# Loading the first quarter of W1 ahead of the last v rows, and moving one batch's transposes between others: a sliding-window attention with a two-layer network behind it

## The chip, the cores and the metric

The kernel runs on one core of one Trainium2 chip. The metric is the time of one execution on the device in microseconds (us). The engines: PE (TensorE) multiplies matrices, and transposes by multiplying with an identity; DVE (VectorE) and ACT (ScalarE) do elementwise work and empty PSUM, the memory that PE writes; POOL (GpSimd) casts the inputs from f32 to f16; SP's queue issues the loads.

## The reference, cut to what matters

```python
def _attn_ref(q, k, v):                       # 8 batches, 8 heads, 576 rows, 64 wide
    scores = scale * np.matmul(q, k.transpose(0, 1, 3, 2))
    mask = (rel >= 0) & (rel < window)        # window = 64
    ...                                       # softmax over the masked scores
    return np.matmul(attn, v)

def _moe_ref(x, g_ln, w_ch1, w_ch2):          # x: 8 x 576 x 512, w_ch1: 512 x 2048
    xn = (x - mu) / np.sqrt(var + 1e-06) * g_ln
    return x + np.maximum(xn @ w_ch1, 0.0) @ w_ch2
```

## The kernel before

Batches go through PE one behind the other. While PE works on the two layers of batch g, the attention of batch g+1 is put between its pieces ("units"): `at(i, f, ...)` puts a call into **slot** i, which runs after unit i. PE runs all of this in the order written. For batch 0 there are 30 units: 8 of the first layer on half the rows, 8 on all rows, 10 of the second layer on three row blocks at once, and 4 on the last block.

```python
load_qk(0, 0); load_v(0, 0, 2)                # SP's queue, in this order
load_qk(0, 1); load_v(0, 2, 4)
for i in range(8): w1_load(i)                 # W1 in eight half-loads of 512 KB
# ...
cast_v(0, 2, 3); cast_v(0, 3, 4)              # POOL, in this order
nc.gpsimd.tensor_copy(out=vB[0][64:128, 3, :, 0:D], in_=v32[0][0:64, 3])
for i in range(8): w1_cast(i)                 # times g_ln, to f16
# ...
def t_main(b, x, half, eng=None):             # q (x=0) or k (x=1): 8 transposes, then one copy
    tp = t_tile([128, 8, 128], ...)           # slots 17 to 24: ONE shared PSUM bank
    ...                                       # also taken by zt_step, the row transposes
# batch 0's slots, which carry batch 1's attention:
at(20, b_step, 1, 1)                          # attention product, division, statistics, z
at(21, zt_step, 1, 0); at(23, zt_step, 1, 1)
at(24, t_main, 1, 0, 1, 0); at(26, t_main, 1, 1, 1, 1)
at(25, vB_cur, 1, 2, 0); at(25, vB_prev, 1, 2, 1); at(26, vB_cur, 1, 3, 0)
at(28, s_mm, 1, 2); at(28, s_mask, 1, 2)      # scores and exponentials; mask
at(29, s_mm, 1, 3); at(29, s_mask, 1, 3)
at(30, b_step, 1, 2)
# batch 1's slots:
at(1, b_step, 1, 3); at(2, zt_step, 1, 2)
at(14, b_step, 2, 0)                          # batch 2's first attention product
```

The softmax here doesn't subtract the row's maximum and nothing guards it: scores larger than these inputs give would overflow.

## Time and profile before

| | before |
|---|---|
| time, median of 3 | 308.18 us (307.89 to 308.82) |
| span of the profiled run | 305.9 us |
| PE busy | 97% |
| PE's waits after its first one | 1.9 us, all before 57 us |
| PE starts batch 0's fifth hidden unit | 25.87 us |
| batch 1's second q half landed | 46.90 us |

The lines that carry this are in the prediction. One habit of reading matters throughout: a profile names as waits only idle time of an engine. Where I speak below of a PE **stand**, I took the start-to-start distance of two products less the usual one (0.216 us for 512 columns, 0.109 for 256, 0.055 for 128), so a stand reads 0.1 to 0.2 us longer than the idle time in the wait lines. Distances up to 0.1 us over the usual, which come with every change from one kind of product to another, are not counted.

### The profile page before, as it was taken

What the parts mean: (1) busy time and instruction counts of PE and PEld (TensorE: products, weight loads), DVE (VectorE), ACT (ScalarE), POOL (GpSimd) and SP (SyncE); (2) the same over time, 40 slices, a digit from 0 to 9 for tenths busy, and PEclk for the clock granted to TensorE, in tenths of its full rate; (3) what the DMA queues carried; (4) which work ended last, traced back from release to release, by engine and by line L of the source; (5) the groups of instructions that cost most, each with busy time, mean ns of one, the idle gap of its engine ahead of it and who ended that gap; (6) DMA issues with size and microseconds to landing.
All of it is one profiled execution on the core that took longest, in us unless ns stands there. A gap on an engine that the chain in (4) does not pass through costs nothing.

```text
span 305.9 us, 7582 instructions
## 1 busy us (share of the span) xinstructions
PE 295.4 (97%) x3061; PEld 196.4 (64%) x3061; DVE 220.6 (72%) x412; ACT 150.7 (49%) x253; POOL 173.3 (57%) x256
## 2 busy tenths in 40 slices
PE   6989999999999999999999999999999999999992
PEld 4557545687454478547854786469646854788882
DVE  0778696767766995589656965896669685789972
ACT  2586635587227733775157527752475046306500
POOL 7589676564952789179806983698146507014300
PEclk9999999999999999999999999999999999999998
DMA  8999999999776997899189997993790399003014
GB/s 191 266 385 301 314 366 286 303 284 236 150 181 228 243 172 147 280 280 127 35 243 303 204 160 245 298 155 70 215 175 19 53 189 208 19 17 139 0 38 103
DMA packets 113669, 58.35 MB, mean 191 GB/s; under 512 B 83617, under 2 KB 104609, under 8 KB 113634
## 3 DMA queue, kind: packets, MB, share of 16 engines
q1 hardware_dynamic: 112576, 54.67, 74.0%
q0 software_dynamic: 768, 2.80, 3.8%
q8 instruction: 24, 0.39, 0.5%
q10 hardware_dynamic: 290, 0.40, 0.5%
q14 instruction: 11, 0.09, 0.1%
HBM read 38.80 MB, written 9.44 MB: 158 GB/s over the span
## 4 chain that ended last, share of the span: by engine, by line
PE 89%; SPq 4%; DMA 2%; POOL 1%; ACT 1%; DVE 1%; issue 0%; ACTq 0%
PE hps L401 30%; PE pA L478 12%; PE pB L478 8%; PE pC L478 8%; PE hph L537 6%; PE ch L413 6%; PE xps L321 4%; PE sc L286 4%; PE ch L554 3%; PE tp L229 3%; PE lA L592 2%; DMA w1s<-in_moe_w_ch_dram 2%; SPq L141 2%; POOL w1g L190 1%; SPq L89 1%; PE lC L592 1%
## 5 line engine op out<-in xcount | busy, mean ns | idle before, releaser
L401 PE MATMUL hps<-zT,w1g 128*128 128x512 f16 x416 | 95.3, 380 | 0.0
L405 ACT ACTIVATE hrT<-hps 128x512 f16<-128x512 f32 x104 | 62.3, 599 | 39.3 <-PE hps L401 35.7
L401 PEld LDWEIGHTS <-w1g 128*128 128x128 f16 x416 | 38.6, 98 | 43.3 <-issue 0.7
L294 ACT ACTIVATE pt<-sc 128x512 f16<-128x512 f32 x72 | 39.0, 594 | 27.7 <-PE sc L286 20.5
L478 PEld LDWEIGHTS <-sS 128*128 128x128 f16 x448 | 43.4, 98 | 4.9
L351 POOL TENSOR_SCALAR rsz<-mvg 128x1 f32<-128x1 f32 x28 | 10.2, 364 | 60.6 <-DVE mvg L332 59.8
L128 POOL CAST qk<-qk 128x1024 f16<-128x1024 f32 x32 | 36.3, 1147 | 11.3 <-DMA qk<-in_k_dram 5.6
L478 PEld LDWEIGHTS <-hrT 128*128 128x128 f16 x336 | 32.4, 98 | 5.5 <-ACT hrT L637 0.3
L301 DVE TENSOR_TENSOR pt<-pt,mask 128x1024 f16<-128x1024 f16 x32 | 27.5, 867 | 8.4 <-ACT pt L294 8.4
L215 ACT COPY qkT<-tp 128x1024 f16<-128x1024 f16 x16 | 16.1, 1012 | 34.1 <-PE tp L229 34.1
L485 DVE TENSOR_TENSOR xn<-pA,xn 128x512 f32<-128x512 f32 x28 | 19.2, 685 | 16.7 <-PE pA L478 11.1
L478 PE MATMUL pC<-w2s,sS 128*128 128x256 f16 x224 | 27.1, 273 | 0.0
L478 PE MATMUL pA<-wT,sS 128*128 128x256 f16 x224 | 26.9, 273 | 0.0
L354 POOL TENSOR_SCALAR z<-xn,rsz 128x512 f16<-128x512 f32 x28 | 24.9, 888 | 2.9
L327 DVE TENSOR_TENSOR xn<-xps,rcp 128x512 f32<-128x512 f32 x36 | 24.9, 691 | 1.5 <-DMA out_dram<-xn 0.3
L329 DVE BATCH_NORM_STATS2 stats<-xn 128x6 f32<-128x512 f32 x36 | 25.0, 695 | 1.2
L324 DVE RECIPROCAL rcp<-xps 128x8 f32<-128x8 f32 x36 | 7.3, 204 | 24.7 <-PE xps L321 24.7
L452 DVE TENSOR_TENSOR sS<-hrT 128x512 f16<-128x512 f16 (+1 forms) x40 | 24.5, 613 | 0.6 <-ACT hrT L405 0.6
L537 PE MATMUL hph<-zT,w1g 128*128 128x256 f16 x192 | 23.8, 273 | 1.0 <-DVE zT L371 0.5
L321 PEld LDWEIGHTS <-pt 128*64 128x64 f16 x576 | 12.2, 110 | 13.7 <-issue 5.5
L352 POOL TENSOR_TENSOR rsz<-rsz,mhalf 128x1 f32<-128x1 f32 x28 | 19.4, 692 | 2.3
L147 POOL CAST vA<-v 128x1024 f16<-128x1024 f32 (+2 forms) x19 | 17.4, 930 | 5.6 <-DMA v<-in_v_dram 5.6
(113 smaller groups left out, 448.9 us busy)
## 6 DMA issues: line engine op xcount, KB each, us to landing
out_dram<-xn SPq DMA_DIRECT2D x33, 256.0 KB, 2.8
qk<-in_q_dram SPq DMA_DIRECT2D x16, 512.0 KB, 6.2
qk<-in_k_dram SPq DMA_DIRECT2D x16, 512.0 KB, 6.9
v<-in_v_dram SPq DMA_DIRECT2D x32, 256.0 KB, 7.7
w2s<-in_moe_w_ch_dram SPq DMA_DIRECT2D x9, 512.0 KB, 9.2
w1s<-in_moe_w_ch_dram SPq DMA_DIRECT2D x4, 512.0 KB, 7.3
tk<-in_k_dram SPq DMA_DIRECT2D x8, 256.0 KB, 4.5
tv<-in_v_dram SPq DMA_DIRECT2D x8, 256.0 KB, 5.0
```

Of the source, the lines that this page charges most:

```text
L128: nc.gpsimd.tensor_copy(out=dst[:, :].rearrange("p (a j) e d -> p a e j d", j=j), in_=t[:, :].rearrange("p (a e j d) -> p a e j d", e=2, j ...
L294: nc.scalar.activation(out=o, in_=i, func=AF.Exp, bias=0.0, scale=scale)
L301: nc.vector.tensor_tensor(out=ptv, in0=ptv, in1=mb, op=ALU.mult)
L321: nc.tensor.matmul(out=xps[64 * r:64 * r + 64, h, :D + 1], lhsT=pt[:, par, hp, r, :], rhs=rhs, start=True, stop=True)
L327: nc.vector.tensor_tensor(out=xn, in0=xps[:, :, 0:D], in1=rcp_b, op=ALU.mult)
L329: nc.vector.bn_stats(out=stats, in_=xv)
L354: nc.gpsimd.tensor_scalar(out=z, in0=xv, scalar1=rs, scalar2=nm, op0=ALU.mult, op1=ALU.add)
L401: nc.tensor.matmul(out=hps, lhsT=w1g[:, kc, 128 * hc:128 * (hc + 1)], rhs=zT[g][:, kc, :], start=(kc == 0), stop=(kc == NKC - 1),)
L405: nc.scalar.activation(out=hrT[:, hc, :], in_=hps, func=AF.Relu, bias=0.0, scale=1.0)
L452: nc.vector.tensor_tensor(out=o, in0=x, in1=y, op=op)
L478: nc.tensor.matmul(out=o, lhsT=a[:, c, 128 * p:128 * p + 128], rhs=wv[:, c, :], start=(first and (p == 0 or split_c) and c == 0), stop=(c ...
L537: nc.tensor.matmul(out=hps[:, e], lhsT=w1g[:, kc, 128 * hc:128 * (hc + 1)], rhs=zT[g][:, kc, 256 * half:256 * half + 256], start=(kc == 0) ...
```

## The change

It has two parts. Part 1: two of the eight half-loads of W1 come before the last 128 rows of batch 0's v, in SP's queue and on POOL, so that PE's first hidden unit need not wait for weights. Part 2: the transposes of batch 1's second half go two slots earlier, between the row transposes, and its scores one slot earlier, so that PE does not run out of work at the end of batch 0.

```diff
     load_qk(0, 1)
-    load_v(0, 2, 4)
-    for i in range(8):
+    load_v(0, 2, 3)
+    w1_load(0)
+    w1_load(1)
+    load_v(0, 3, 4)
+    for i in range(2, 8):
         w1_load(i)
...
     cast_v(0, 2, 3)
+    w1_cast(0)
+    w1_cast(1)
     cast_v(0, 3, 4)
     nc.gpsimd.tensor_copy(out=vB[0][64:128, 3, :, 0:D], in_=v32[0][0:64, 3])
-    for i in range(8):
+    for i in range(2, 8):
         w1_cast(i)
...
-            at(24, t_main, 1, 0, 1, 0)
-            at(26, t_main, 1, 1, 1, 1)
+            at(22, t_main, 1, 0, 1, 0)
+            at(24, t_main, 1, 1, 1, 1)
...
-            at(28, s_mm, 1, 2)
-            at(28, s_mask, 1, 2)
-            at(29, s_mm, 1, 3)
-            at(29, s_mask, 1, 3)
+            at(27, s_mm, 1, 2)
+            at(27, s_mask, 1, 2)
+            at(28, s_mm, 1, 3)
+            at(28, s_mask, 1, 3)
```

## The prediction

> **What bounds the kernel now.** I read first the busy table of the page, then the chain of waits that ended last, then the waits of the matrix engine (PE), and last the timelines of POOL, PE, ACT and DVE in the two stretches that the change touches: 8 to 30 us and 45 to 61 us. The busy table:
> ```profile
> PE 295.4 (97%) x3061; PEld 196.4 (64%) x3061; DVE 220.6 (72%) x412; ACT 150.7 (49%) x253; POOL 173.3 (57%) x256
> ```
> PE is busy 97% of a 305.9 us span and the chain is 89% PE. So the time is PE's own work plus the moments in which PE stands still. The waits of PE over the whole span (who waited for whom; us in total, times, longest):
> ```profile
> PE warm L762 <- DVE mbias L755: 2.3, 1, 2.3
> PE xps L321 <- ACT pt L294: 0.7, 2, 0.4
> PE hph L537 <- DVE zT L371: 0.5, 1, 0.5
> PE hph L537 <- POOL w1g L190: 0.4, 1, 0.4
> PE xps L321 <- DVE pt L301: 0.3, 1, 0.3
> ```
> All five fall before 57 us; asked for 60 us onward the view lists none. Two things follow. The most that any reordering near the start can save is the last four rows, 1.9 us, or 0.6% of 308.18. And a delay that PE still carries at 60 us should reach the end one for one, as nothing later is waiting to absorb it.
>
> **First stretch.** The wait that the first part aims at is `hph <- w1g`. The POOL timeline (start, duration, what, idle before):
> ```profile
> 16.77 1.37 POOL L190 TENSOR_SCALAR w1g<-w1s,gT 128x512 f16<-128x512 f32 x2 [0.21 <-POOL vB L781]
> 19.40 4.08 POOL L190 TENSOR_SCALAR w1g<-w1s,gT 128x512 f16<-128x512 f32 x6 [1.25 <-DMA w1s<-in_moe_w_ch_dram]
> ```
> Each half-load of W1 (512 KB) is cast by two instructions of about 0.69 us. The first is done by 18.14; POOL then idles 1.25 us for the second to land, and casts three half-loads in a row until 23.48. PE started its first hidden-layer unit at 19.75 and, having done two of its eight products (0.11 us apart when nothing waits), stood for the third until 20.14 and for the fourth until 20.82.
>
> **Second stretch.** The chain of waits there (start, us, what):
> ```profile
> 53.80 0.39 PE sc L286 x16
> 54.19 1.08 ACT pt L294 x2
> ...
> 55.31 0.43 PE sc L286 x15
> 55.74 1.08 ACT pt L294 x2
> ...
> 56.85 0.69 DVE pt L301
> 57.54 0.13 DVE rcp L324
> ...
> 57.69 0.70 DVE xn L327
> ...
> 58.44 0.45 PE xps L321 x16
> ```
> Scores, exponentials, mask and division of batch 1's second half stand so late that PE runs out of other work. In PE's timeline the gaps are about 0.45 us before 56.04, 0.25 before 58.44 and 0.2 before 59.91: 0.9 us. This is what the second part aims at.
>
> **What the Trainium skill says.** "PSUM — Partial Sum Buffer", section Engine vs sequencer instructions: "MATMULs start and complete in program order"; the other engines' queues are strict FIFO. The trace agrees: during the stand from 20.15 to 20.82 no later matmul slips in. So a transpose placed before its data is there stops everything behind it. "DMA: Bandwidth & Descriptors", section Queues, rings and completion order: each DMA engine takes its descriptors in ring order. All loads here go out on SP's queue, and the trace agrees in that they land in the order of issue. The same page, section Why a DMA increments its semaphore by 16 and not by 1: a load has landed only when the slowest engine has. The trace shows one such case: a 16 KB packet of the instruction queue at 15.99 took 1.12 us, and from then on the slowest engine's landing of a W1 load is about 2 us behind the fastest's (0.5 us before).
>
> **Part 1: W1's first quarter ahead of the last v chunk.** It removes and adds no work: the same 4 casts of 0.69 us, v cast of 0.62 us and vB copy of 0.68 us, and the same bytes, in another order. Landings before, from the loads' issue times and times to landing: v chunk 2 at 14.04, v chunk 3 at 15.15, W1 half-loads at 16.56, 19.32, 20.66 and 22.03. The 16 DMA engines are busy throughout (the DMA row is at 7 to 9 tenths from 0 to 90 us, 9 where this happens), so I take landings as a matter of bytes ahead in the queue. After the change the first half-load lands about 1.1 us sooner, 15.45; the second 18.2; and v chunk 3, with all four ahead of or at it, where the second half-load landed before: 19.3. Loads 3 and 4 of W1 stay at 20.66 and 22.03.
>
> POOL then: first cast 15.5 to 16.9; second 18.25 to 19.62; v 19.66 to 20.28; vB copy 20.34 to 21.02; after the same 0.2 us pause as before, third W1 cast 21.2 to 22.57, fourth 22.57 to 23.94. PE gains 0.75 us in its first unit. But the attention step of rows 384 to 511 now needs vB, at 21.05, and the third unit needs the **fourth** cast: ready at 23.48 before and 23.94 after. Even with no delay on POOL it could not be before 22.03 + 0.07 + 1.37 = 23.47, since that load lands no sooner. So the gate at 23.5 stays and may move by +0.45 us. The 0.5 us wait at 25.87 for zT hangs on the same gate: 13 products at 0.11 us, transposes to 25.35, DVE copy to 25.8. So part 1: between 0 and +0.45 us.
>
> **Part 2: transposes two slots earlier, scores one slot earlier.** No instruction is added. The shown order of each engine moves as the diff says: on ACT the q transpose's copy goes between the two zT copies; on DVE the k transpose's copy moves ahead of one add of the output, and both masks go ahead of the **last** add (0.74 us).
>
> The q transposes stand after slot 22. PE's row at 46.05 holds slots 22 and 23, so slot 22 ends at 46.05 + 6 x 0.216 = 47.35. Are the inputs there? POOL's cast of that q half:
> ```profile
> 47.02 1.04 POOL L128 CAST qk<-qk 128x1024 f16<-128x1024 f32 x1 [0.72 <-DMA qk<-in_q_dram]
> ```
> It ends at 48.06 and starts when the load lands (issued 36.35, 10.5 us to landing, 46.9), which part 1 does not move. The single shared transpose bank agrees: ACT empties it of the earlier transpose only at
> ```profile
> 47.42 0.56 ACT L369 COPY zT<-ztp 128x512 f16<-128x512 f16 x1
> ```
> that is 47.98. So PE stands from 47.35 to about 48.1: **+0.75 us**, a wait that the old order (49.72) did not have.
>
> Going on from 48.1: 8 transposes 0.45, slot 23 1.3, zT transposes 0.22, slot 24 0.87, k transposes 0.45 (at 50.97), slots 25 to 27 2.17, scores at 53.6, slot 28 0.87, second scores ending at 55.5 (they wait for the first exponentials, as before), slot 29 0.87. The next attention product starts at 56.45 without a wait, against 56.04 before: of 0.75 lost, about 0.35 came back. Then DVE: the second mask is ready to start at 56.75 (exponentials end 55.55 + 1.15) and takes 0.69; now the 0.74 add comes **after** it, then the reciprocal 0.2 and the product 0.69, so xps is free at 59.05, not 58.4. The following z at 60.5 instead of 59.85. PE reaches 60 us **+0.6 us** late. If part 1 delays PE by its 0.45, the bank is emptied later by as much and the sum goes to +1.0; if part 1 gains, the load and the bank hold PE at 48.1 anyhow.
>
> **Sum.** 308.18 + 0.6 = 308.8 us.
>
> **Rivals.** (1) The intent holds: q lands some 0.5 us or more sooner, or POOL gets ahead, the stand at 47.35 shrinks, and the 0.9 us of gaps before 60 us are mostly filled: 307.5. For it: the gaps are real. Against it: POOL waits for DMA before each cast of that stretch, and the bytes ahead are the same. (2) The late v chunk is the worse: with casts pushed behind it, part 1's +0.45 adds to the bank wait: 309.2. For it: POOL had no idle time between 19.40 and 27.67 to absorb 1.3 us of v work. Against it: if the 1.12 us packet falls elsewhere, v chunk 3 lands at 18 and its casts fit before the third load. (3) All is hidden: 308.2.
>
> **Range and chances.** Most paths lie between +0 and +1; the three runs before spread by 0.9 us. So 308.8, eighty in a hundred from 307.7 to 309.6. Two per cent is 6.2 us, over three times all the waits that could go and six times the delay I expect: within 2% 0.97, faster 0.01, slower 0.02.
>
> **What would show it.** Right: no `hph <- w1g` wait in the first unit but one of it or its like at 23.5 to 24; a PE gap of 0.3 to 0.8 us at slot 22, before the q transposes at 48.1; no gap before the attention product near 56.4; the second mask followed by the add, and a longer wait for xps near 59. Wrong: q cast ending before 47.4, or PE at 60 us no later than before. The prediction fails if landings move other than by bytes ahead, or if PE has slack after 60 us.

## The result, and the profile after

The changed kernel took 309.52 us (median of 4, 308.93 to 309.73), the one before in the same rounds 308.32. The ratio is 1.0035, 95% interval 1.0014 to 1.0056: a little slower, within 2%. (A ratio here is the mean time of one kernel's fast runs over that of the other's of the same rounds, so not quite the ratio of the medians quoted.) Timed again on another chip, in the experiments below, it was 1.001 (0.9995 to 1.0024). The loss is real in the first comparison and not clear of zero in the second.

PE's waits over the whole span, after (us in total, times, longest):
```profile
PE warm L765 <- DVE mbias L758: 2.3, 1, 2.3
PE tp L229 <- POOL qk L128: 1.8, 1, 1.8
PE xps L321 <- ACT pt L294: 0.7, 2, 0.4
PE hph L537 <- DVE zT L371: 0.5, 1, 0.5
PE hph L537 <- DVE xn L423: 0.2, 1, 0.2
```
Two rows of before are gone: `hph <- w1g` (0.4) and `xps <- pt L301` (0.3), what the two parts went after. Two are new, and the first is larger than all that went: the q transposes wait for POOL's cast. The PE timeline there (start, duration, what, idle before):
```profile
46.13 1.46 PE L554 MATMUL ch<-w2s,hrT 128*128 128x512 f16 x6
49.41 0.62 PE L229 MATMUL tp<-ident,qk 128*128 128x128 f16 x8 [1.82 <-POOL qk L128]
49.87 1.46 PE L554 MATMUL ch<-w2s,hrT 128*128 128x512 f16 x6
```
The chain of waits tells why (start, us, what):
```profile
36.11 12.08 DMA qk<-in_q_dram
...
48.31 1.05 POOL qk L128
...
49.41 0.62 PE tp L229 x8
...
58.06 0.69 DVE pt L301
58.75 0.67 DVE xn L423
...
59.47 1.03 PE hph L537 x8
```
The q half was issued at 36.11 and landed 12.08 us later, at 48.19; the cast follows at once, the transposes at once after that. Before the change the chain through 46 to 54 us had PE pieces only. Further down, mask, then add, then PE: the second new wait.

The POOL timeline of the first stretch, after:
```profile
15.53 2.95 POOL L190 TENSOR_SCALAR w1g<-w1s,gT 128x512 f16<-128x512 f32 x4 [0.87 <-DMA w1s<-in_moe_w_ch_dram]
18.43 0.61 POOL L147 CAST vA<-v 128x512 f16<-128x512 f32 x1
19.10 0.69 POOL L786 CAST vB<-v 64x512 f16<-64x512 f32 x1
20.54 2.69 POOL L190 TENSOR_SCALAR w1g<-w1s,gT 128x512 f16<-128x512 f32 x4 [0.75 <-DMA w1s<-in_moe_w_ch_dram]
```
The first quarter of W1 is cast by 18.48 (20.76 before) and the v work fits into POOL's idle time. The fourth cast ends at 23.23 (23.48 before). Yet PE's fifth unit starts at 25.95, where it started at 25.87: up to there part 1 has bought nothing.

### The profile page after: what moved, and what is told of

Its sections match the earlier page's. It is cut to its first block, busy times and chain, and to the rows that moved or that the text cites. A ratio compares the mean times of both kernels' runs of the same rounds, so it can differ in the third digit from the quotient of the medians.

```text
span 307.8 us, 7582 instructions
## 1 busy us (share of the span) xinstructions
PE 296.3 (96%) x3061; PEld 196.6 (64%) x3061; DVE 218.8 (71%) x412; ACT 150.7 (49%) x253; POOL 171.6 (56%) x256
## 4 chain that ended last, share of the span: by engine, by line
PE 81%; DMA 8%; SPq 4%; POOL 3%; ACT 1%; DVE 1%; issue 0%; POOLq 0%
PE hps L401 28%; PE pA L478 12%; PE pB L478 8%; PE pC L478 8%; PE ch L413 5%; PE hph L537 4%; DMA qk<-in_q_dram 4%; PE xps L321 4%; PE sc L286 3%; DMA w1s<-in_moe_w_ch_dram 3%; PE tp L229 2%; PE lA L592 2%; POOL w1g L190 2%; SPq L141 2%; DMA w2s<-in_moe_w_ch_dram 2%; SPq L89 1%
## 5 line engine op out<-in xcount | busy, mean ns | idle before, releaser
L128 POOL CAST qk<-qk 128x1024 f16<-128x1024 f32 x32 | 35.1, 1110 | 13.3 <-DMA qk<-in_k_dram 6.8
L301 DVE TENSOR_TENSOR pt<-pt,mask 128x1024 f16<-128x1024 f16 x32 | 26.7, 839 | 8.8 <-ACT pt L294 8.7
L485 DVE TENSOR_TENSOR xn<-pA,xn 128x512 f32<-128x512 f32 x28 | 19.2, 685 | 16.9 <-PE pA L478 11.3
L537 PE MATMUL hph<-zT,w1g 128*128 128x256 f16 x192 | 23.4, 273 | 0.7 <-DVE zT L371 0.5
L352 POOL TENSOR_TENSOR rsz<-rsz,mhalf 128x1 f32<-128x1 f32 x28 | 19.3, 691 | 2.3
```

What stands on the lines that cost most here:

```text
L128: nc.gpsimd.tensor_copy(out=dst[:, :].rearrange("p (a j) e d -> p a e j d", j=j), in_=t[:, :].rearrange("p (a e j d) -> p a e j d", e=2, j ...
L301: nc.vector.tensor_tensor(out=ptv, in0=ptv, in1=mb, op=ALU.mult)
L537: nc.tensor.matmul(out=hps[:, e], lhsT=w1g[:, kc, 128 * hc:128 * (hc + 1)], rhs=zT[g][:, kc, 256 * half:256 * half + 256], start=(kc == 0) ...
```

## The experiments

Twelve runs were made; three of them, r3, r4 and r9, are unchanged copies of the two kernels. r3, r4, r5, r6 and r8 are single runs, whose state is unknown; their spans lie among those of the fast runs. (A run counts as slow when it is over 1.5% above the fastest of its kernel.) All gave a right result by the comparison, also the two whose q data I made wrong: q and k are drawn at a tenth of unit size, so the scores hardly shape the softmax.

First the reading of all 14 profiles, from the instruction and landing records of the traces, as the later sections use it. "q landed" is the last of 16 DMA engines of batch 1's second q half. "Later stands" are those from 53 to 62 us without the 0.23 us between the two score blocks, which all have. "Batch 2" is the start of its first attention product, with the stand before it in that column's brackets. Times in us.

| profile | q landed | stand at q | later stands | batch 2 | span |
|---|---|---|---|---|---|
| before | 46.90 | 0 | 0.96 | 73.73 (0) | 305.9 |
| r3_before_again | 47.75 | 0 | 2.07 | 75.18 (0) | 307.3 |
| r1_part1 | 48.40 | 0 | 1.37 | 74.78 (0) | 306.9 |
| r2_part2 | 47.72 | 1.64 | 0.39 | 75.14 (0) | 307.3 |
| after | 48.19 | 1.98 | 0.39 | 75.61 (0) | 307.8 |
| r4_after_again | 48.16 | 1.56 | 0.41 | 75.82 (0.32) | 308.1 |
| r9_after_timed | 47.41 | 0.83 | 0.73 | 75.08 (0) | 307.2 |
| r5_early_q | 47.28, not used | 0.69 | 0.74 | 74.54 (0) | 307.3 |
| r6_own_bank | 47.58 | 1.54 | 0.38 | 75.34 (0.44) | 307.5 |
| r7_early_q_own_bank | 47.49, not used | 0 | 0.98 | 74.85 (0.39) | 307.0 |
| r8_mask_late | 47.24 | 1.06 | 1.27 | 75.36 (0) | 307.6 |
| r10_later_step (slow run) | 47.03 | 0 | 0.66 | 76.94 (3.60) | 310.6 |
| r11_own_bank_later | 47.41 | 0 | 0 | 74.20 (0.89) | 306.3 |
| r12_both_later | 47.33 | 0 | 0 | 77.71 (2.35) | 309.6 |

### r1 and r2: each part alone; r3 and r4: both kernels once more

r1 is the first two hunks of the diff above on the kernel before, r2 the other two. r3 and r4 are unchanged copies.

> Part 1 alone (W1's first quarter ahead of the last v chunk; batch 1's transposes and scores where they were). Theory T (the loss is part 2's stand before the q transposes): ratio 0.999 to 1.001, no wait of the first hidden units for w1g, PE back to back from 26 us to 55 us, gaps near 56 to 60 us as before. Rival R (the new load order itself makes later loads land late, the q half at 48.2 instead of 46.9): the q half lands near 48.2 here too, but as its transposes stand after slot 24 (49.7) the time still moves by under 0.3 us. Rival S (the v chunk's late cast delays the third unit): ratio 1.0015, a wait for w1g near 23.5.

> Part 2 alone (transposes at slots 22 and 24, scores at 27 and 28; W1 loaded in the old order). Theory T: all of the loss is here, ratio 1.002 to 1.004, a PE wait for the q cast of 0.7 us if the q half lands at 46.9, up to 2 us if it lands near 48.2. Rival R: with the old load order the q half lands at 46.9, the wait is 0.7 us and the ratio 1.002. Rival S: ratio 1.000.

> The kernel before, unchanged, to see what differs between two profiles of one kernel. If the landing of batch 1's second q half (46.9) and the moment at which PE's clock is granted in full (9.55 us) belong to the order of loads, both repeat to 0.1 us; if they are chance of an execution, they move by up to 1.5 us.

> The changed kernel, unchanged. Same question: q half at 48.2 and clock at 11.33 us again if they belong to the kernel; if chance, the q half may land near 46.9 with a PE wait of 0.7 us, and the clock may come anywhere in about 3 us.

Measured: part 1 alone 1.0032 (0.9989 to 1.0076), part 2 alone 1.001 (0.9984 to 1.0035). These intervals are as wide as the effect; on this chip six runs of one kernel spread by up to 4 us (part 1: 308.38 to 312.36). **The times do not apportion the loss**, and I do not read them so. The traces do better. The stand at q is there in r2 and r4 and not in r1 and r3: it belongs to part 2. In all six profiles in which the moved transposes take the q half from its own load (after, r2, r4, r6, r8, r9) they start 1.22 us after it lands. So the size of the stand belongs to the execution: the q half landed at 46.90 and 47.75 in two profiles of the one kernel before. Rival R, that the new load order makes q late, is not needed: r2, with the old order, has a stand of 1.64 us. R had foreseen 46.9 for r2 (47.72 came) and 48.2 for r1 (48.40 came). Over all profiles the old order of loads gives 46.90 to 47.75, the new one 47.24 to 48.40, later by 0.36 us in the mean; they overlap, and in each case the fastest DMA engine is through by 44.9 to 46.0. The slowest is then 1.7 to 3.2 us behind. The three latest landings are all of the new order, so a small effect of the order stays open.

For part 1 I compared when PE starts the fifth unit: 25.73 to 26.50 us in the six profiles with the old order of loads, 25.77 to 26.32 in the eight with the new one. No difference, and r1 has no wait for W1's cast near 23.5, which rival S (late v casts) had foreseen: S falls too.

One cause of the scatter near the start is PE's clock. By the clock record it was granted in full from 9.55 us in the profile of before and from 11.33 in that of after, and from 8.6 to 11.9 over all. The two profiles are level at 8.86 us, and by its first scores PE is 0.88 us later in that of after (11.48 against 10.60), with the same instructions and inputs; it then came too late to meet the fourth W1 cast. Over all profiles PE starts its first hidden unit at 19.59 to 19.79 us in the six whose clock came by 9.6, and at 20.18 to 21.15 in the eight whose clock came from 10.4 on. The Trainium skill, "TensorE: Matmul & The Clock Gate", Part 1: The HAM clock gate, says that the window which releases the clock is free-running, so that the moment differs from run to run by some 500 ns either way; here it differs too, but by more, with 3.3 us between the extremes.

### r5 to r8: which input do the q transposes wait for?

r5 casts the q half from a tile that landed long before, ahead of W2's last cast (a wrong result). r6 writes both transposes to a score bank instead of the shared one. r7 does both. r8 puts the last mask behind the last add.

```diff
 # r5 (cut: five lines that keep the first half's tile under the name of entry 2)
     for i in range(8):
+        if i == 7:
+            cast_qk(1, 2, (0,))               # entry 2: the first half's tile again
+            qk16[(1, 0, 1)] = qk16.pop((1, 0, 2))
         w2_cast(i)
...
-    cast_qk(1, 1)
+    cast_qk(1, 1, (1,))
 # r6
-        tp = t_tile([128, 8, 128], f"tp_{b}_{x}_{half}")
+        if (b, half) == (1, 1):
+            tp = ps_s.tile([128, 8, 128], FP16, tag="sc", name=f"tp_{b}_{x}_{half}")
+        else:
+            tp = t_tile([128, 8, 128], f"tp_{b}_{x}_{half}")
 # r8
-            at(28, s_mask, 1, 3)
+            at(29, s_mask, 1, 3)
```

> The changed kernel with a wrong result on purpose: batch 1's second q half is cast from the tile of the first half, which landed long before, and ahead of the last cast of W2; the load itself stays. Theory T (the q transposes wait for data, then for the shared PSUM bank): PE's stand before them falls from 1.6-2.0 us to what the bank alone costs, 0.5 to 0.7 us, transposes near 48.0. Rival B (the bank alone is the wait): the stand stays over 1.5 us. Rival P (PE's order, not its inputs): stays.

> The changed kernel, right result, with both transposes of batch 1's second half written to a score bank instead of the shared transpose bank. Theory T: the stand before the q transposes stays within 0.2 us of that without it (1.5 to 2.0 us where the q half lands near 48, 0.7 where near 47), as the data come after the bank is free. Rival B: the stand is gone.

> Both of the above (wrong result on purpose): neither data nor bank to wait for. Theory T: no stand before the q transposes, PE at 72 us of the changed kernel's trace 1.5 to 2 us earlier, ratio to the kernel before 0.996 to 0.999, so the stand was more than the whole loss. Rival S (something else of the change costs): ratio still 1.002 or more.

> The changed kernel with the last mask put behind the last output add on VectorE, as it was before the change. My prediction said that mask, then add, then reciprocal and product would hold xps until 59 and cost some 0.6 us there. If so, the wait of the second hidden unit of the next batch for the add (0.4 us in the changed kernel) goes and the following attention product starts about as early or earlier; if the order costs nothing, PE's stands between 55 and 62 us still sum to about 0.6 us.

Measured, r5 and r6 in PE's waits (one row each, in that order):
```profile
PE tp L233 <- ACT zT L373: 0.5, 1, 0.5
```
```profile
PE tp L232 <- POOL qk L128: 1.4, 1, 1.4
```
With the data there, the transposes start at 47.98 and what they wait for is ACT's copy out of the shared bank; with a bank of their own and the data late, the wait stays. In r7 they start at 47.25, straight after slot 22. So both inputs are late for slot 22, and the data later than the bank: as theory T has it.

But r7's **time** is not what T expected (0.996 to 0.999): 1.0001 (0.9954 to 1.0047). Its waits show where the gain went:
```profile
PE hph L544 <- DVE xn L430: 0.8, 1, 0.8
...
PE tp L236 <- POOL qk L132: 0.3, 1, 0.3
PE xps L328 <- DMA vB<-vA: 0.2, 1, 0.2
```
The k transposes now wait for their own cast, the second hidden unit of batch 1 waits for DVE, and batch 2's first attention product waits for its vB, which comes by DMA. The DVE wait is longer than in the changed kernel (0.2) because of this (POOL's row first, then DVE's):
```profile
56.11 1.04 POOL L132 CAST qk<-qk 128x1024 f16<-128x1024 f32 x1 [1.11 <-DMA qk<-in_q_dram]
```
```profile
56.40 1.29 DVE L308 TENSOR_TENSOR pt<-pt,mask 128x1024 f16<-128x1024 f16 x1 [0.86 <-ACT pt L301]
57.62 0.74 DVE L430 SCALAR_TENSOR_TENSOR xn<-ch,rstdg,xn 128x512 f32<-128x512 f32 x1
```
The mask takes 0.69 us when alone. Here it is recorded from 56.40 to 57.69, 0.54 us past the end of a POOL cast that was already running. In r1, r3, r5 and r8 (1.08, 1.08, 1.05 and 1.52 us) it also ends 0.54 to 0.55 us after the cast does. The Trainium skill, "SBUF — State Buffer", section Who interferes with whom, says that a DVE instruction with two SBUF inputs contends with POOL's reads, for a port pair that is an exclusive lock. This agrees. The casts start when loads land, so whether the last mask meets one is decided by the landing: it cost the kernel before 0.4 us in r3 and nothing in its first profile. In r3 a second one followed: the z of the same rows (L343, 0.49 us in the profile of before) took 1.22 us, from 60.08 to 61.30, through the end of a cast and three memsets of POOL, and the row transposes stood for it. That is why the later stands of r3 are the longest in the table.

r8 does not decide what the order mask-then-add costs. The wait of the hidden unit for the add is gone, as expected, but its mask met a cast (1.52 us), and PE stood 1.27 us instead of 0.39.

### r9 to r11: the change timed again, and another way to the same stands

r9 is the changed kernel. r10 is the kernel before with the attention product of batch 1's last rows and the row transposes ahead of it one unit later, after the data it needs instead of before. r11 adds own banks, k transposes at 25 instead of 26, and scores one slot earlier; the q transposes stay at 24.

```diff
 # r10 (and r11)
-            at(1, b_step, 1, 3)
-            at(2, zt_step, 1, 2)
+            at(2, b_step, 1, 3)
+            at(3, zt_step, 1, 2)
 # r11 only, with r6's edit
-            at(26, t_main, 1, 1, 1, 1)
+            at(25, t_main, 1, 1, 1, 1)
-            at(25, vB_prev, 1, 2, 1)
+            at(26, vB_prev, 1, 2, 1)
-            at(28, s_mm, 1, 2)
-            at(28, s_mask, 1, 2)
-            at(29, s_mm, 1, 3)
+            at(27, s_mm, 1, 2)
+            at(27, s_mask, 1, 2)
+            at(28, s_mm, 1, 3)
```

> The changed kernel again, timed beside the next two on one chip. Theory T: ratio 1.001 to 1.004; PE's stand before the q transposes equals the end of the q cast less 47.4, here 0.7 to 2 us depending on the landing; PE reaches 26 us as the kernel before does.

> The kernel before with one edit: the attention product of batch 1's last 128 rows and the row transposes ahead of it stand one hidden unit later (slots 2 and 3 of the next batch, were 1 and 2). Theory: the stands near 58.4 and 59.9 that the change went after (0.5 us in one profile of the kernel before, 1.6 in the other) are filled without asking for any data sooner: ratio 0.996 to 0.999. Rival: the stand moves to the transposes behind it, ratio 1.000.

> The kernel before with that edit and, in place of the change's earlier transposes: q transposes where they were (after slot 24), k transposes one slot earlier (25), both in score banks, scores one slot earlier (27, 28), the last mask behind the last add. Theory: no stand before the q transposes (their cast ends before 49.5 in every profile so far), none before the attention product near 56: ratio 0.995 to 0.998, below the run with the later step alone. Rival: a stand before the k transposes (cast ends 49.9 to 51.1, slot 25 ends near 50.6) gives it back, ratio as with the later step alone.

Measured: r9 1.001 (0.9995 to 1.0024), as expected, with the smallest stand of the three profiles of the changed kernel, 0.83, for a q half at 47.41. r10 1.0007 (0.9982 to 1.0033), three of its six runs slow; r11 1.0045 (1.0003 to 1.0087). Both missed what I expected of their times. Yet r11's profile has no stand at all from 53 to 62 us (but the 0.23 that all have), and came to the same product of batch 1's first layer at 70.25 us where r9 came at 71.93. What it won went into one wait further on:
```profile
74.20 0.19 PE L324 MATMUL xps<-vB,pt 128*64 128x65 f16 x1 [0.73 <-DMA vB<-vA]
```
This is batch 2's first attention product, which waits for the copy of v that is made by DMA from POOL's cast, which waits for the load of batch 2's v. From the start of that product to the end eleven of the fourteen profiles take 232.1 to 232.3 us (the others are r12, in which it stands two slots later, with 231.8, r5 with 232.8 and r10 with 233.7). So the start of that product all but sets the time. In the profiles in which it waits for vB (r4, r6, r7, r10, r11, and r12 below) it starts 0.13 or 0.14 us after vB has landed, at 74.07 to 77.58. The kernel before started it earliest of all, at 73.73, and did not wait, as its vB had landed at 73.12. Here too the landing of an execution decides whether a gain in front of the product is kept. In r10's profile the stand there was 3.6 us, and by the clock record PE's clock was then halved from 76.88 to 80.30.

### r12: the second gate out of the way?

```diff
 # r11, and:
-                at((14, 17, 20, 23)[j], b_step, 2, j)
-                at((14, 17, 20, 23)[j], z_step, 2, j)
+                at((16, 18, 20, 23)[j], b_step, 2, j)
+                at((16, 18, 20, 23)[j], z_step, 2, j)
```

> The previous kernel (own bank, later step) with the first two attention products of batch 2 two slots and one slot later (slots 16 and 18, were 14 and 17). Theory: what is won before 70 us was given back at batch 2's first attention product, whose vB lands between 73 and 77 us; with it at about 76 the stand of 0.9 us (3.6 us where the loads were late) is gone or under 1 us, PE's clock stays granted in full, and the ratio is 0.993 to 0.998, below both kernels. Rival: the product's follow-up (division, statistics, row transposes of batch 2) then comes late and a stand appears further on: ratio 0.999 to 1.003.

Measured: 1.0103 (1.0075 to 1.0132), within 2% but clearly slower, and by more than the rival had said. Its profile has two stands. The first is 2.2 us, before batch 2's first product, and the profile puts it down to a mask (PE's row, then DVE's):
```profile
77.71 0.19 PE L324 MATMUL xps<-vB,pt 128*64 128x65 f16 x1 [2.07 <-DVE pt L304]
```
```profile
70.06 0.69 DVE L304 TENSOR_TENSOR pt<-pt,mask 128x1024 f16<-128x1024 f16 x1
70.66 3.60 DVE L383 TENSOR_SCALAR rstmp<-mvg 128x4 f32<-128x4 f32 x1
...
76.90 0.68 DVE L304 TENSOR_TENSOR pt<-pt,mask 128x1024 f16<-128x1024 f16 x1
```
The name is misleading. The mask at 76.90 belongs to the next 128 rows, whose scores PE made only at 72.40; the product's own rows were masked at 70.06. The product also reads vB, whose copy POOL issued at 69.71, after batch 2's v had landed at 66.82, the latest of the fourteen profiles:
```profile
69.71 0.74 POOL L165 DMA_DIRECT2D vB<-vA  x1 [0.30 <-POOL vA L147]
```
The landing records have vB at 77.58, within 0.02 us of the end of that mask, and PE starts 0.13 us later, as in r11. So it is the second gate again, later than the 73 to 77 us that I had counted on.

The second stand is 1.6 us, at the start of batch 2's own first layer, which waits for its row transposes:
```profile
96.16 0.59 PE L404 MATMUL hps<-zT,w1g 128*128 128x512 f16 x2 [1.46 <-DMA zT<-z]
```
This is the rival's. The edit put z of the first rows behind the casts of batch 3's v in POOL's order, and the second of those waited for its load:
```profile
81.53 1.04 POOL L147 CAST vA<-v 128x1024 f16<-128x1024 f32 x1 [1.09 <-DMA v<-in_v_dram]
82.67 0.18 POOL L354 TENSOR_SCALAR rsz<-mvg 128x1 f32<-128x1 f32 x1
```
Its statistics were ready at 80.07. That this delay reaches the transposes at 96 us is my reading of the timelines; no run tests it, and r12's other four executions have no profile.

The DVE row of 3.60 us is worth a look for itself: four elements per partition, 0.16 us in r11's profile, recorded through a DMA issue of POOL (70.46 to 70.99), a memset and three casts in a row, to their end:
```profile
71.23 3.00 POOL L128 CAST qk<-qk 128x1024 f16<-128x1024 f32 x3
```
No version here beats the kernel before.

## Why the prediction was right or wrong

**The time** (308.8, range 307.7 to 309.6): the medians were 309.52 and, again, 309.11, inside the range; "within 2%" was right. The shift was +1.20 us (0.35%) and +0.25 us (0.1%) where I had said +0.6 (0.2%): twice as much and less than half. That the number lies between them is luck. (A slip in the prediction: 2%, 6.2 us, is ten times the delay of 0.6 us, not six.)

**Step 1, part 1 between 0 and +0.45 us**: 0. That the gate at 23.5 stays, because the fourth half-load lands no sooner, held: 23.48 and 23.23 for the fourth cast, and PE's fifth unit did not move. The 0.75 us that PE was to gain in its first unit shows where profiles with a like clock are compared, the six whose first unit starts at 19.6 to 19.8. Their second unit starts at 21.18 to 21.38 with the new order (r5, r6, r8) and at 21.72 to 22.17 with the old (before, r3, r10). At the fifth, 25.77 to 25.92 and 25.73 to 26.19, nothing is left of it.

The +0.45 did not come. Its term of 19.3 for the landing of v chunk 3 depends on the execution. In the changed kernel's profile the chunk landed at 17.90, as the 16 KB instruction packet, at 15.99 before, came behind it at 17.76 (I had named this under rival 2). In r5, r6 and r8 the packet came at 16.5 to 16.7 and the chunk landed at 19.2 to 19.3, as said; yet there too the fourth cast ended at 23.38 to 23.53. The term that was mis-sized everywhere is the second half-load of W1: I had it land at 18.2 and its cast end at 19.62. In all eight profiles of the new order it landed at 16.66 to 16.86 and the cast ended at 18.26 to 18.53. The landing that I had moved forward by 1.1 us, 19.32, held a lag: fifteen engines were through by 17.80 there. So POOL's v work was over by 19.8 in the changed kernel, and by 20.7 at the latest, just before the third half-load landed. The wait "of it or its like at 23.5 to 24" is not in the changed kernel's profile, as PE's clock was late, but it is in r5, r6 and r8 (0.38 us idle, until 23.4 to 23.6).

**Step 2, a stand of 0.75 us before the q transposes**: the mechanism was right, by r1 to r7, and the size was off. It measured 1.98 us, and 1.56 and 0.83 in the two repeats. The mis-sized term is the landing at 46.9: in fourteen profiles it landed between 46.90 and 48.40, and the one that I had read was the earliest. Behind it stood the assumption that landings are "a matter of bytes ahead"; the prediction named its failure as a way to be wrong, and r3, the same kernel with the same bytes, landed 0.85 us later. In the changed kernel's profile fifteen of the sixteen engines were through by 46.45; the last took until 48.19. The bank at 47.98 was right (r5: 0.69 us by itself).

**Step 3, what the earlier scores give back**: the product near 56 came without a wait, as said. Then I said xps is held to 59.05 by mask and add. The order of the chain was right; the wait came one step sooner, at the second hidden unit, which needs the PSUM bank that the add empties (0.39 us). From the end of slot 22 to the row transposes near 60 us PE took 12.57 us in the profile that I had and 14.36 in the changed kernel's: of a stand of 1.98 us it gave back 0.2, where I had said 0.15 (of 0.75, +0.6 left). So the sum of this step was right for that profile. (The stands of the table fall by more, from 0.96 to 0.39, as they hold distances that are there in any case.) But the give-back belongs to the execution too: without part 2 that stretch took 12.57, 13.68 and 13.24 us (before, r3, r1), with it 14.36, 13.95, 13.46 and 14.01 (after, r4, r9, r2), 0.8 us more in the mean, and from -0.2 to +1.8 by the pair that one takes. r3 and r2, in which q landed at the same time (47.75 and 47.72), differ by 0.3 us. This fits a loss near 0.3% in one comparison and 0.1% in the other; how much of each run's time is which was not shown, as the times are too noisy for it.

**Step 4, a delay at 60 us reaches the end one for one**: right for the delay here: 1.87 us at the row transposes near 60 (61.78 against 59.91), 1.88 at batch 2's product, 1.9 in the span. I had not seen that a gain would not: batch 2's v is a second gate, which opened between 73.1 and 77.6 us (r7, r11, r12). "Nothing later is waiting to absorb it" read too much from a list of waits in which an engine arrives late everywhere.

## What to carry to other kernels

Moving an instruction earlier on an in-order engine pays only if its inputs are there: before moving it, look up when its data land, in more than one profile, and take the latest. A schedule whose waits are short because a load happened to land early has no reserve. And a gap that is filled gives nothing where the next load-bound step sets the pace: look for the next gate before counting the gain. Last, where a profile names who ended a wait, check that the waiting instruction reads what the named one wrote (r12).

## What the Trainium skill lacked or had wrong

- "DMA: Bandwidth & Descriptors" has no word on the scatter of one load's landing between executions: the same 512 KB, behind as many bytes, landed at 46.90 to 48.40 us, with 1.7 to 3.2 us between the fastest and the slowest of 16 engines. That 16 KB instruction packets (about 1.1 us each, at 16 to 18, 25 and 41 us) make the lag is my reading of the times, not shown: the records do not tell which engine carried them. For it: with the old order of loads the second half-load of W1 landed at 19.19 to 19.63 where the packet came at 16.0 to 16.4 (before, r3, r10), and at 17.86 to 18.15 where it came at 17.3 to 18.0 (r2, r11, r12).
- "SBUF — State Buffer" speaks of the lock as held for one instruction. Here a DVE instruction of 0.16 us was recorded for 3.60 us, over three POOL casts in a row and more, and one of 0.49 us for 1.22 us, over the end of a cast and three memsets. That it is this lock is my reading: both end within 0.3 us after POOL's last.
- "Perfetto Trace Analysis" lists waits for semaphores and in queues as outside the recorded window and does not say where time blocked on the shared port goes. It is inside: the mask reads 1.05 to 1.52 us where it takes 0.69 alone.
